# Attention and a gated feed-forward layer on one core: seven half products for half of gate and value, fixed order lists, and a residual added in DRAM

## The chip, the cores and the metric

The kernel runs on one core of a Trainium2 chip. Its time is the device time of one execution in microseconds (us). The engines are TensorE (PE, with the weight loads shown apart as PEld), VectorE (DVE), ScalarE (ACT), GpSimd (POOL) and SyncE (SP). Each runs its own instructions in program order; they wait for each other through semaphores. DMAs are issued from POOL's and SP's queues.

## The reference, cut to what matters

The first half is attention over 4 batches, 8 heads, 768 tokens and 64 numbers per head. Heads 0, 2 and 6 see all earlier tokens; the others see the first four tokens and a window of 64. The second half takes the result as `x` with 3072 rows of 512 numbers:

```
a = softmax(where(mask, q @ k.T / 8, -1e9)) @ v      # per batch and head
x = a laid out as [3072, 512]
g   = x @ w_gate                                     # [3072, 1536]
val = x @ w_val                                      # [3072, 1536]
ffn = gelu(g) * val @ w_out                          # [3072, 512]
out = x + sigmoid(x @ w_res) * ffn
```

Inputs and outputs are float32. The kernel multiplies in float16 with float32 sums.

## The kernel before

The 3072 tokens are cut into six chunks of 512 (`CHUNKS`); a chunk takes four tiles of 128 tokens, from one or two batches. Each chunk passes through the same stages. Attention writes `xtok` (its rows in float32), and transposes on TensorE give `xT`, the same in float16 with the 512 features on the partitions in four groups. `gate_value` (line 1121) works through 12 blocks `f` of 128 hidden columns. For each it makes gate and value as four matmuls of 512 tokens each into one PSUM bank; ACT then takes the gelu (line 1166) and DVE multiplies it with the value (line 1168) into `hT`. `output_fast` (line 1212) makes the product with `w_out` for pairs of token tiles. It already uses Winograd's scheme: seven products of half size in place of eight, from sums of `hT` blocks that `sums` forms on DVE (line 1187, kept in `hS` and partly over `hT`), and from sums of `w_out` blocks that `weight_sums` forms once (`wt`). Partial results are copied out of PSUM (`keep`, lines 1251 and 1252), added to (`plus`, line 1257), multiplied with the gate made from `x @ w_res` by a tanh (line 1226 and `gated`, line 1281), and added to `xtok` (line 1286). SP then stores a tile of 256 KB (line 1292). The four buffers `otile` (line 508) hold these tiles from the first keep to the end of the store. Chunk 0 does part of its work in plain form.

Attention of one chunk is interleaved with the output of the chunk before it, so TensorE alternates between stages of gate and value alone and stages of the mixed kind.

Each operation is a task of a graph (`Graph`, `schedule` at line 219) with a cost, a priority and the buffers that it needs. A list scheduler runs through modelled time, picks for each engine the ready task with the best priority for which the buffers are free, and so fixes at build time the order of each engine's queue and the place of each buffer. `HINTS` changes the priority of single tasks. Some tasks (`flex`) may go to DVE or ACT. PSUM has eight banks; `P_ps` lists for each kind of use which banks it may take. Matmuls go through a helper `mm`: lines 516 and 517 are the whole array and two halves of 64 columns.

The loads of q, k (64 KB each, transposed on the way in by DMA for some chunks) and v for all batches go through the pools `qks`, `qkt`, `va`, `vs`, `q6` in batches; `qkt` holds the transposed q and k of one batch in one buffer of which there are two.

Of the kernel before, what the change touches and what calls it, by code (L numbers as in the profile page):

```python
# [4 lines left out]
NHEAD = 8  # L5
# [38 lines left out]


HINTS = (
    "3:-58.9 11:-130.04 428:854.14 430:718.61 444:2782.08 457:-821.9 460:407.45 490:4205.68 521:1522.06 "
    "591:-818.43 610:-36.63 612:486.89 613:-2965.25 619:1544.03 621:-44.07 643:467.87 644:-881 646:4.3 656:119.6 "
    "664:25.04 673:629.62 675:-109.25 695:-2674.26 696:-1856.67 703:-881.5 706:-108.75 707:714.39 708:1939.7 "
    "711:270.02 712:497.18 716:476.22 720:652.56 738:638.32 743:520.23 744:3053.24 749:514.3 750:1799.28 "  # L50
    "751:2383.53 756:521.28 762:1469.72 764:4344.87 767:2237.74 787:-603.93 815:5053.25 817:2978.67 821:1231.87 "
    "824:1484.86 836:2402.62 837:798.1 841:706.04 848:-288.52 849:2997.07 876:2751.74 906:2555.54 913:1516.93 "
    "918:2437.99 919:1519.88 924:1537.25 931:1510.23 936:2384.32 949:2443.79 955:2089.28 967:2846.74 995:-227.38 "
    "1001:29.83 1002:3171.86 1003:3180.29 1004:1146.58 1007:2686.58 1012:1781.89 1040:-803.29 1043:1907.45 "
    "1045:1028.83 1046:667.33 1050:3229.28 1051:1536.45 1053:3573.03 1056:-1823.77 1084:4090.27 1110:2454.97 "
    "1111:2597.62 1117:2808.38 1123:2507.5 1128:2481.58 1129:2529.63 1134:2508.5 1146:2434.73 1152:2779.33 "
    "1153:3034.61 1158:3861.94 1165:2795.06 1171:3076.63 1176:2997.8 1185:5989.69 1188:2243.92 1189:2528.84 "
    "1192:2789.39 1193:2537.45 1194:3836.22 1208:3021.15 1215:6294.68 1263:3219.13 1268:5037.38 1283:4420.5 "
    "1308:4756.92 1311:3513.6 1317:3517.03 1321:3052.3 1329:5930.49 1330:3507.5 1335:3508.5 1336:3519.22 "
    "1341:4624.14 1345:3444.6 1353:3516.64 1354:3538.83 1357:2761.66 1365:3787.63 1366:5173.04 1372:5102.72 "  # L60
    "1386:5438.32 1392:4014.31 1393:4933.66 1418:5146.68 1430:4133.91 1441:5428.8 1452:5127.54 1457:2188.42 "
    "1462:4595.33 1464:5711.23 1467:9389.54 1468:4425.54 ~1471:550.69 1476:5611.77 1499:4504.13 1513:6742.83 "
    "1516:5340.27 1522:4510.5 1523:4585.63 1526:3632.38 1534:4503.02 1539:4253.34 1550:4463.64 1565:7711.51 "
    "1570:4506.5 1571:5085.34 1580:2427.42 1594:2466.44 1610:9272.71 1625:3048.93 1627:6036.71 1629:6167.81 "
    "1631:5064.12 1644:6476.5 1662:4125.72 1671:5044.95 1672:7314.6 1676:4967.2 1683:6427.71 1692:9540.12 "
    "1711:7387.16 1757:5137.62 1784:5507.1 1797:5469.41 1803:7562.23 1817:7773.49 1818:7478.69 1823:7672.83 "
    "1834:7419.08 1836:10250.4 1849:7490.55 "
)

# [31 lines left out]
class Buf:  # L101
    __slots__ = ("pool", "kind", "slot", "left", "users", "war", "free_at")

    def __init__(self, pool, kind=None):
        self.pool, self.kind = pool, kind
        self.slot = None
        self.left = 0
        self.users = []
        self.war = []
        self.free_at = 0.0  # L110


class Pool:
# [14 lines left out]

    def take(self, buf, t):
        best = min(x for x in self.free if x[0] <= t)  # L130
        self.free.remove(best)
        buf.slot = best[1]
        buf.war = list(self.last[best[1]])
        self.held.setdefault(buf.kind, []).append(None)
# [9 lines left out]
class Psum:  # L144
# [23 lines left out]

    def take(self, buf, t):
        sp = self.spots(buf.kind, t)[0]  # L170
        buf.slot = sp
        for b in sp:
            self.free[b] = 1e18
        buf.war = [u for b in sp for u in self.last[b]]
        self.held[buf.kind].append(None)
# [15 lines left out]
VS_DMA = 0  # L191
LAT = {"pe": 0.20, "act": 0.10, "dve": 0.08, "pool": 0.12, "sp": 0.1}


class Graph:
# [22 lines left out]

    def schedule(self):
# [21 lines left out]
        running = []  # L241
        while left:
# [3 lines left out]
            for e in ENGS:  # L246
# [3 lines left out]
                for t in cand[e]:  # L250
# [6 lines left out]
                    key = (int(away), p_, t.seq)  # L257
                    if t.ready > now or (best is not None and key >= bkey):
                        continue
                    if t.alts and any(max(free[f], now) + t.alts[f][0] + BIAS[f] < now + t.alts[e][0] + BIAS[e] - 1e-6  # L260
                                      for f in t.alts if f != e):
                        continue
                    need = {}
                    ok = True
                    for b in t.bufs:
                        if b.slot is None:
                            if not b.pool.can(b.kind, now):
                                ok = False
                                break
# [15 lines left out]
                progressed = True  # L285
                if t.name == "g0" and warming:
# [114 lines left out]
    def emit(self):  # L401
# [31 lines left out]
        with nc.Block() as blk:  # L433
# [18 lines left out]
            def _(e):  # L452
                run("sp", e)
                for t in finals:
                    e.wait_ge(t.sem, 16)
# [6 lines left out]
def c_act(n):  # L462
    return 0.19 + n * 0.000834


def c_dve(n, rate=1.0, psum=True):
    return (0.125 if psum else 0.065) + n * 0.00104 / rate
# [6 lines left out]
def build_kernel(nc, q, k, v, w_gate, w_val, w_out, w_res, out):  # L474
# [11 lines left out]
    scratch = sb("scratch", [128, 1], FP16)  # L486
    blank = sb("blank", [128, 128], FP16)
# [4 lines left out]
    P_vs = Pool(many("vs", 2, [128, NT - 1, NHEAD, DHEAD + 1], FP16))  # L492
    P_vk = Pool(many("vk", 2, [128, 8, DHEAD + 1], FP16))
    P_qkt = Pool(many("qkt", 2, [128, 2, NPAIR, SEQ], FP16))
# [9 lines left out]
    P_hs = Pool(many("hS", 1, [128, 3, NF // 2, 2, 128], FP16))  # L504
    wt = sb("wt", [128, 4, NF // 2, 256], FP16)
    P_ga = Pool(many("gact", 4, [128, 512], FP16))
    P_sr = Pool(many("srs", 3, [128, 512], FP32))
# [5 lines left out]
    def mm(e, o, lhsT, rhs, **k):  # L513
# [8 lines left out]
        "gv": (4, one(6, 7, 5, 4, 3, 2)), "gv0": (4, one(6, 7, 5, 4)), "gvh": (4, one(7, 6, 4, 5)), "out": (2, one(6, 7)), "fin": (4, one(6, 7, 1, 0)), "warm": (1, one(7, 5)),  # L522
# [55 lines left out]

    wtok = {}

    def load_weights():
# [6 lines left out]
        for j in range(4):  # L588
# [3 lines left out]
            wtok["o", j].late = 2.2  # L592
        for nm in "gv":
            for j in range(3):
                wtok[nm, j].late = 2.2 if j else 2.0
# [8 lines left out]
    def batch(b):  # L604
        if b not in batches:
            B_ = B()
            B_.v, B_.vs, B_.vk, B_.qkt = Buf(P_v), Buf(P_vs), Buf(P_vk), Buf(P_qkt)
# [4 lines left out]
        return batches[b]  # L612

    def values(b, a, z, base, each, on_engines=False):

        BB = batch(b)
        for i in range(a, z):
            BB.vtok[i] = dma("pool", base, 0.9, (lambda i=i: lambda: at(BB.v)[:, i, :, 0:DHEAD])(),
                             v[b, :, i * 128:(i + 1) * 128, :].rearrange("h p d -> p h d"), bufs=[BB.v])
            BB.vtok[i].late = 1.6 if base < 50 else 6.0  # L620
        if a == 0:
# [9 lines left out]
            for t in BB.vktok:  # L631
                t.slack = 12.0 if b else 0.0
# [5 lines left out]
        if on_engines:  # L638
            ts = []
            for lo, hi, pr in ((1, 2, -75),) + (() if VS_DMA else ((2, 4, 130),)):  # L640
                for dst, src, off in ((0, 64, 1), (64, 0, 0)):
                    def vs(on, dst=dst, src=src, off=off, lo=lo, hi=hi):
                        def fn(e):
                            o = at(BB.vs)[dst:dst + 64, lo - 1:hi - 1, :, :].rearrange("p i h d -> p (i h d)")
                            i_ = at(BB.v)[src:src + 64, lo - off:hi - off, :, :].rearrange("p i h d -> p (i h d)")
                            return e.activation(out=o, in_=i_, func=AF.Copy) if on == "act" else e.tensor_copy(out=o, in_=i_)
                        return fn
                    n_ = (hi - lo) * 520
# [9 lines left out]
        for lo in cuts:  # L658
            hi = lo + 1 if each else z
            ts = []  # L660
            for dst, src, off in ((0, 64, 1), (64, 0, 0)):
                ts.append(G.add("sp", 1.2, (lambda lo=lo, hi=hi, dst=dst, src=src, off=off: lambda e: e.dma_start(
                    at(BB.vs)[dst:dst + 64, lo - 1:hi - 1, :, :].rearrange("p i h d -> p (i h d)"),
                    at(BB.v)[src:src + 64, lo - off:hi - off, :, :].rearrange("p i h d -> p (i h d)")))(),
# [7 lines left out]
    def loads_rows(c, si, b, a, z):  # L672
# [27 lines left out]
        per = 1 if c == 0 or n == 4 else 2  # L700
        for k_ in range(0, NPAIR, per):
            ps_ = ORDER[k_:k_ + per]
            pr = 1000 * c - 492 + ps_[0] if c else 40 * k_ - 205
            for js in (((1,), (0,)) if c == 0 else ((0, 1),)):
                scr = Buf(P_ps, "scr" if c else "scr0")
                items = [(p, jj) for jj in js for p in ps_]
# [10 lines left out]
                def ev(on, p0=ps_[0], scr=scr, j0=js[0], m=len(items)):  # L717
                    def fn(e):
                        o = at(BB.qkt)[:, :, :, lo:hi].rearrange("c j (y x) w -> c x (j y) w", x=2)[:, p0 % 2]
                        m0 = j0 * 2 + p0 // 2  # L720
                        o = o[:, m0:m0 + m, :].rearrange("c m (p j) -> c m p j", j=n)
# [5 lines left out]
                           bufs=[scr, BB.qkt], name="qkE")  # L727
# [4 lines left out]
    def loads_natural(c, si, b, a, z):  # L732
# [8 lines left out]
        for i in range(a, z):  # L741
            for j, src in ((1, k), (0, q)):
# [9 lines left out]
                for d in ds:  # L752
                    d.late = 5.0
                t = G.add("sp", 1.65, (lambda sv=sv, i=i, j=j: lambda e: e.dma_start(
                    at(BB.qkt)[:, j, :, i * 128:(i + 1) * 128], sv(), transpose=True))(), ds, base, bufs=[st, BB.qkt], dma=0.85, name="dT")
# [4 lines left out]
            if i == a:  # L760
                values(b, a, z, base, False)
        t = G.add("sp", 0.8, lambda e: e.dma_start(at(BB.q6)[0:64, :, a * 128:z * 128], at(BB.qkt)[64:128, :, 1, a * 128:z * 128]),
                  loaded, base + 1, bufs=[BB.qkt, BB.q6], dma=0.4, name="q6")
        t.late = 1.0
        copies.append(t)
        for i in range(a, z):
            BB.q6tok[0, i] = BB.q6tok[1, i] = t
# [90 lines left out]
    def scores(P, tiles, banks, g, retr):  # L858
# [7 lines left out]
        for bi, (x, blocks, low) in enumerate(banks):  # L866
# [3 lines left out]
            for (b, kt, q0, nq) in blocks:  # L870
# [5 lines left out]
                if kt is None:  # L876
                    deps += [BB.ktok[p, q0]] + ([BB.ktok[p, q0 - 1]] if q0 else [])
                    parts = [(max(0, q0 * 128 - 64 + 64 * s), q0 * 128 + 64 * s, 64, o + 64 * s) for s in range(2)]
                else:
                    deps.append(BB.ktok[p, kt])  # L880
                    parts = [(kt * 128, q0 * 128, nq * 128, o)]
                for i in range(nq):
                    P.where[x, kt, b, q0 + i] = w_ + i * 128
                for (k0, qq, w, oo) in parts:
                    mms.append((lanes[lane], len(mms), BB, half, k0, qq, w, oo, low))
# [5 lines left out]
        def sc(e):  # L891
            side = lambda BB, low, j: at(BB.q6)[:, j, :] if low else at(BB.qkt)[:, j, p, :]
            return [e.matmul(at(scr)[:, oo:oo + w], lhsT=side(BB, low, 1)[half, k0:k0 + 128],  # L893
                             rhs=side(BB, low, 0)[half, qq:qq + w], start=True, stop=True)
                    for (_, _, BB, half, k0, qq, w, oo, low) in mms]
# [549 lines left out]
```

The softmax here doesn't subtract the row's maximum and nothing guards it: scores larger than these inputs give would overflow.

## Time and profile before

| what | value |
| --- | --- |
| median of three runs | 265.6 us (265.23, 265.60, 265.98) |
| span of the profiled execution | 263.7 us; the page gives no other time for it, so the median of the runs lies 1.9 us above its span |
| TensorE busy | 257.7 us (98%), 3226 instructions |
| VectorE busy | 181.6 us (69%), 378 instructions |
| ScalarE busy | 147.2 us (56%), 237 instructions |
| GpSimd busy | 89.3 us (34%), 127 instructions |
| first and last gate matmul stages begin at | 19.72 us (chunk 0), 224.85 us (chunk 5) |
| stages of gate and value of chunks 1 to 5 begin at | 63.7, 105.2, 143.9, 184.3, 224.9 us |
| DMA moved | 29.22 MB |

An engine's share of the span is an average; the table of 40 slices in the profile tells where in time it lies. A row of a group gives busy time and mean of one instruction, then the idle time of the engine just before it and what ended most of it. A line of the time view gives start, duration, engine, line, operation, output and inputs. A row of a tile or of a line of code adds the time from issue of a DMA to its landing.

### The profile page before, as it was taken

To read this page: it belongs to the slowest core of one execution; us is meant where nothing else is said; L and a number is where in the kernel's file an instruction comes from. 1 tells how busy PE (TensorE), PEld (TensorE's weight loads), DVE (VectorE), ACT (ScalarE), POOL (GpSimd) and SP (SyncE) were. 2 spreads that over 40 slices of the span, in tenths; PEclk is the share of its full clock that TensorE was granted. 3 is DMA by queue.
4 is the path that set the end of the run, shared out by engine and by line. 5 is a ranking of instruction groups with operands and counts; after the bars stand their busy time and mean duration, and the time that the engine had idled before them with its cause. 6 is when DMAs were issued, how large, how long until landed. Compare 5 with 4: busy or idle time off the path is not lost.

```text
span 263.7 us, 7495 instructions
## 1 busy us (share of the span) xinstructions
PE 257.7 (98%) x3226; PEld 164.0 (62%) x3226; DVE 181.6 (69%) x378; ACT 147.2 (56%) x237; POOL 89.3 (34%) x127
## 2 busy tenths in 40 slices
PE   7999999999999999999999999999999999999993
PEld 6777655468444668544567444589655588655692
DVE  2698437798447888557898366888557689837655
ACT  2785467974244987423787242967243888233430
POOL 8999979506109973975000000000000000000003
PEclk9999999999999999999999999999999999999999
DMA  6999999999999999999996110004200004200003
GB/s 83 174 204 206 188 175 231 175 153 204 134 200 148 165 137 177 171 179 176 174 156 150 42 40 0 2 26 101 82 2 0 2 2 122 82 2 0 2 35 127
DMA packets 96513, 29.22 MB, mean 111 GB/s; under 512 B 84449, under 2 KB 93025, under 8 KB 96481
## 3 DMA queue, kind: packets, MB, share of 16 engines
q0 software_dynamic: 70320, 14.69, 67.5%
q1 hardware_dynamic: 26160, 14.07, 28.0%
q8 instruction: 25, 0.41, 0.7%
q14 instruction: 8, 0.06, 0.1%
HBM read 29.36 MB, written 6.29 MB: 135 GB/s over the span
## 4 chain that ended last, share of the span: by engine, by line
PE 95%; DMA 2%; DVE 1%; issue 0%; POOLq 0%
PE ps L516 50%; PE ps L517 32%; PE ps L893 5%; PE ps L1333 2%; PE ps L1017 2%; PE ps L709 2%; DMA qks<-in_q_dram 2%; PE ps L1106 2%; PE ps L984 1%; DVE otile L1281 1%; DVE otile L1286 1%; DVE otile L1257 0%; POOLq L1427 0%
## 5 line engine op out<-in xcount | busy, mean ns | idle before, releaser
L1166 ACT ACTIVATE gact<-ps 128x512 f16<-128x512 f32 x68 | 40.2, 597 | 73.5 <-PE ps L516 43.7
L1168 DVE SCALAR_TENSOR_TENSOR hT<-gact,ps 128x512 f16<-128x512 f16 x68 | 46.1, 686 | 48.0 <-PE ps L516 23.1
L516 PE MATMUL ps<-xT,wg 128*128 128x512 f16 (+1 forms) x208 | 50.0, 363 | 0.0
L516 PE MATMUL ps<-xT,wv 128*128 128x512 f16 (+1 forms) x202 | 49.0, 362 | 0.0
L1286 POOL TENSOR_TENSOR otile<-otile,xtok 128x256 f32<-128x256 f32 x3 | 2.4, 801 | 136.2 <-DVE otile L1281 136.2
L577 POOL DMA_DIRECT2D qks<-in_k_dram x36 | 28.0, 810 | 17.3 <-DMA qkt<-qks 13.9
L516 PEld LDWEIGHTS ps<-xT,wg 128*128 128x128 f16 x208 | 20.1, 98 | 20.0 <-DVE otile L1257 0.3
L516 PEld LDWEIGHTS ps<-xT,wv 128*128 128x128 f16 x202 | 19.4, 98 | 20.0 <-DVE hT L1168 0.5
L577 POOL DMA_DIRECT2D qks<-in_q_dram x36 | 28.4, 828 | 2.2 <-issue 1.4
L517 PE MATMUL ps<-xT,wv 128*64 128x512 f16 x204 | 28.3, 380 | 0.0
L577 POOL DMA_DIRECT2D va<-in_v_dram x24 | 21.3, 920 | 15.1 <-PE ps L516 15.1
L517 PE MATMUL ps<-xT,wg 128*64 128x512 f16 x192 | 26.3, 379 | 0.0
L909 ACT ACTIVATE ea<-ps 128x1024 f16<-128x1024 f32 (+2 forms) x24 | 21.1, 915 | 1.7 <-PE ps L893 1.6
L1257 DVE TENSOR_TENSOR otile<-otile,ps 128x256 f32<-128x256 f32 x33 | 13.6, 417 | 7.1 <-PE ps L517 4.7
L1226 ACT ACTIVATE srs<-ps 128x512 f32<-128x512 f32 x22 | 13.1, 595 | 9.1 <-PE ps L517 6.7
L517 PEld LDWEIGHTS ps<-xT,wv 128*64 128x64 f16 x204 | 11.5, 110 | 9.8 <-DVE hT L1168 0.3
L1084 DVE TENSOR_TENSOR xtok<-ps,rcp 128x512 f32<-128x512 f32 (+1 forms) x28 | 16.8, 606 | 0.2
L517 PEld LDWEIGHTS ps<-xT,wg 128*64 128x64 f16 x192 | 11.1, 110 | 9.0
L893 PE MATMUL ps<-qkt 64*128 64x64 f16 (+4 forms) x391 | 16.4, 213 | 0.0
L893 PEld LDWEIGHTS ps<-qkt 64*128 64x128 f16 x391 | 9.8, 94 | 8.0 <-issue 4.2
L516 PE MATMUL ps<-wo,hT 128*128 128x256 f16 (+1 forms) x84 | 14.4, 304 | 0.0
L1286 DVE TENSOR_TENSOR otile<-otile,xtok 128x512 f32<-128x512 f32 (+1 forms) x21 | 14.3, 691 | 0.2
(109 smaller groups left out, 437.4 us busy)
## 6 DMA issues: line engine op xcount, KB each, us to landing
out_dram<-otile SPq DMA_DIRECT2D x22, 256.0 KB, 2.4
va<-in_v_dram POOLq DMA_DIRECT2D x24, 128.0 KB, 17.6
qks<-in_k_dram POOLq DMA_DIRECT2D x32, 64.0 KB, 12.6
qks<-in_q_dram POOLq DMA_DIRECT2D x32, 64.0 KB, 13.0
wg<-in_moe_w_gate_dram POOLq DMA_DIRECT2D x3, 512.0 KB, 10.2
wv<-in_moe_w_val_dram POOLq DMA_DIRECT2D x3, 512.0 KB, 12.1
wo<-in_moe_w_out_dram POOLq DMA_DIRECT2D x4, 384.0 KB, 22.8
vs<-va SPq DMA_DIRECT2D x4, 260.0 KB, 7.9
```

The lines of the kernel that those rows point to most:

```text
L516: return e.matmul(o, lhsT=lhsT, rhs=rhs, **k)
L517: return [e.matmul(o[h:h + 64], lhsT=lhsT[:, h:h + 64], rhs=rhs, **k) for h in (0, 64)][-1]
L577: return G.add(eng, issue, lambda e: e.dma_start(out_ap(), in_ap), deps, prio, bufs=bufs, dma=cost, name=name, grp=grp)
L709: return [e.transpose(out=at16(scr)[64 * x:64 * x + 64, (m * n + i) * 128:(m * n + i + 1) * 128], in_=piece(jj, h, i), identity=ident[:, : ...
L893: return [e.matmul(at(scr)[:, oo:oo + w], lhsT=side(BB, low, 1)[half, k0:k0 + 128], rhs=side(BB, low, 0)[half, qq:qq + w], start=True, sto ...
L909: return e.activation(out=o, in_=i_, func=AF.Exp, scale=SM_SCALE)
L1084: t2 = G.add("dve", c_dve(2 * n * 64), lambda e: e.tensor_tensor(out=xview(), in0=avv(0, DHEAD), in1=scale(), op=ALU.mult), [t1] + xdeps, ...
L1166: ta = G.add("act", c_act(512), (lambda gb=gb, ga=ga: lambda e: e.activation(out=at(ga)[:, :], in_=at(gb)[:, :], func=AF.Gelu))(), [tg], p ...
L1168: th = G.add("dve", c_dve(512), (lambda vb=vb, ga=ga, f=f: lambda e: e.scalar_tensor_tensor(out=hv(f), in0=at(ga)[:, :], scalar=0.5, in1=a ...
L1226: tas.append(G.add("act", c_act(512), (lambda rb=rb, sr=sr: lambda e: e.activation(out=at(sr)[:, :], in_=at(rb)[:, :], func=AF.Tanh, scale ...
L1257: return G.add("dve", c_dve(256), lambda e: e.tensor_tensor(out=dst(), in0=dst(), in1=at(D)[:, 0:256], op=ALU.add), [t, k], pr, bufs=[D, o ...
L1286: fn = (lambda ot=ot, lt=lt, w=w: lambda e: e.tensor_tensor(out=at(ot)[:, w], in0=at(ot)[:, w], in1=at(xbuf)[:, lt, w], op=ALU.add))()
```

## The change

The scheme of seven half products that `output_fast` uses for `w_out` is also used for half of gate and value in chunks 1 to 5. Blocks 6 to 11 form pairs (6,9), (7,10), (8,11), for gate and for value: six products per chunk. The left side is `xT` cut into two halves of 256 tokens and two halves of 256 features, the right side a pair of weight blocks. In place of 16 matmuls of 256 tokens (8 of 512) a pair takes 14 matmuls of 256 tokens. The partial results lie in a "lane", two neighbouring PSUM banks; there are three lanes. A product is a chain of groups of matmuls (`t15`, `t6`, `t7`, `t23`, `t4`), two copies (`seed` in PSUM, `hold` to an `otile` buffer) that may go to DVE or ACT, and two additions on DVE (`merge`). Gelu and product then read both halves. Four sums of `xT` per chunk (`xS`) and eight sums of weights, once (`gv_sums`), are made on DVE.

Further parts:

- `PLAN` holds an explicit order of the tasks for each of the five engines and a place for each buffer; the scheduler follows it and no longer uses `HINTS`. Costs in the model (`c_act`, `c_dve`) have other numbers.
- In chunks 1 to 4 (`ACCUM`) `x` is stored by SP (`store_x`, 1 MB per chunk in one DMA), and the gated tiles are added to it in DRAM by accumulating DMAs on POOL's queue. The 16 DVE adds and 16 SP stores of these chunks go. Chunk 5 adds on the chip as before, and chunk 0 too.
- `qkt` becomes `kT` per batch and `qT` per chunk; a copy `q6` on SP becomes two. `vs` no longer holds head 0. `wt` has three slabs in place of four, `srs` two buffers in place of three. `hS` is split in two. Warm-up matmuls on a zero tile at the start are 256 wide in place of 128.
- In the built program TensorE loses 240 matmuls of 512 columns and gains 420 of 256. DVE instructions go from 378 to 452, ACT from 225 to 281, POOL from 123 to 141, SP from 80 to 73.

The core of the diff:

```diff
+NP = 3
+FA, FB = NF - 2 * NP, NF - NP
+LANES = 3
-HINTS = ( ... )
+PLAN = ( ... )
+ACCUM = range(1, 5)
...
+        lists = [[int(x) for x in line.split()] for line in "".join(PLAN).split("/")] if PLAN else []
+        queue = {e: [self.tasks[x] for x in xs] for e, xs in zip(ENGS, lists)}
...
+                b.fixed = x if x >= 0 else None
...
+                offers = cand[e]
+                if queue:
+                    offers = [t for t in queue[e][heads[e]:heads[e] + 1] if t in offers] + [t for t in offers if t.name == "warm"][:1]
...
-    P_qkt = Pool(many("qkt", 2, [128, 2, NPAIR, SEQ], FP16))
+    P_kt = Pool(many("kT", 2, [128, NPAIR, SEQ], FP16))
+    P_qt = Pool(many("qT", 2, [128, NPAIR, 512], FP16))
...
+        "lane": (LANES, [(4, 5), (2, 3), (0, 1)]),
...
+    def fast(c, xtbuf, xttoks, h, toks, hv, lanes_):
...
+        s1 = add(lambda: S(0), lambda: A(1, 0), lambda: A(1, 1), ALU.add, xd, [xs, xtbuf])
+        s2 = add(lambda: S(1), lambda: S(0), lambda: A(0, 0), ALU.subtract, [s1] + xd, [xs, xtbuf])
+        s3 = add(lambda: xs3[:, :, :], lambda: A(0, 0), lambda: A(1, 0), ALU.subtract, xd + xs3_last, [xtbuf])
+        s4 = add(lambda: S(2), lambda: A(0, 1), lambda: S(1), ALU.subtract, [s2] + xd, [xs, xtbuf])
...
+            lane = lanes_[q % LANES]
+            ps, free = lane
+            es = Buf(P_ot)
...
+                    mm(e, at(ps)[:, D], lhsT=right[r](k), rhs=left[l](k), start=first and k == 0, stop=(k == 1), skip_group_check=True)
+                    for l, r, D, first in parts for k in range(2)], need + deps, p_, bufs=[ps, xtbuf, xs] + list(extra), name=name)
...
+            t15 = product([("A11", "B11", AL, True), ("S1", "T1", AR, False)], list(free))
+            seed = copy((lambda ps=ps: at(ps)[:, BL]), (lambda ps=ps: at(ps)[:, AL]), [t15], [ps], "seed")
+            hold = copy((lambda es=es: at(es)[:, 0:256]), (lambda ps=ps: at(ps)[:, AR]), [seed], [ps, es], "hold")
+            t6 = product([("S2", "T2", BL, False)], [seed])
+            m1 = merge(AR, [t6, hold])
+            t7 = product([("S3", "T3", BL, False)], [m1])
+            t23 = product([("A12", "B21", AL, False), ("S4", "B22", AR, False)], [m1])
+            m2 = merge(BR, [t7])
+            t4 = product([("A22", "T4", BL, False)], [m2])
...
+    def store_x(c, xbuf, xtoks):
+        n = 2 if c == len(CHUNKS) - 1 else 4
+        r0 = c * 512
+        stored[c] = G.add("sp", 0.65, lambda e: e.dma_start(
+            out[r0:r0 + n * 128, :].rearrange("(i p) d -> p i d", p=128), at(xbuf)[:, 0:n, :]),
...
+            if c in ACCUM and not end:
+                t = G.add("pool", 1.0, (lambda ot=ot, r0=r0: lambda e: e.dma_start(out[r0:r0 + 128, :], at(ot)[:, :], accum_op=ALU.add))(),
+                          ends + [stored[c]], pr - 3000, bufs=[ot], dma=1.0, name="out")
+                continue
```

## The prediction

> **What bounds the kernel now.** I read the page first (shares, slices, chain), then the busy time of each engine stage by stage, then the order of TensorE's work in time, then how long DMAs take from issue to landing.
>
> ```profile
> span 263.7 us, 7495 instructions
> PE 257.7 (98%) x3226; PEld 164.0 (62%) x3226; DVE 181.6 (69%) x378; ACT 147.2 (56%) x237; POOL 89.3 (34%) x127
> PE   7999999999999999999999999999999999999993
> PEclk9999999999999999999999999999999999999999
> DMA  6999999999999999999996110004200004200003
> ...
> PE 95%; DMA 2%; DVE 1%; issue 0%; POOLq 0%
> ...
> L1257 DVE TENSOR_TENSOR otile<-otile,ps 128x256 f32<-128x256 f32 x33 | 13.6, 417 | 7.1 <-PE ps L517 4.7
> ...
> out_dram<-otile SPq DMA_DIRECT2D x22, 256.0 KB, 2.4
> ```
>
> TensorE is busy in every slice but the first and last, at the full granted clock, and the chain that ends last is 95% TensorE. The DMA engines are full for the first 21 of 40 slices (to about 138 us) and nearly idle afterwards: DMAs added early meet a full queue, those added late do not.
>
> Busy time by stage: columns are window, length, then PE, PEld, DVE, ACT, POOL with counts, clock, DMA share, GB/s. The first is attention of chunk 2 with output of chunk 1, the second gate and value of chunk 5.
>
> ```profile
> 84.80:105.20 20.40, 20.37 (x300) 14.21 (x300) 17.17 (x40) 17.35 (x25) 14.72 (x21) 1.00 2.05 155
> 224.90:246.70 21.80, 21.80 (x216) 12.12 (x214) 13.71 (x23) 7.14 (x13) 0.00 (x0) 1.00 0.07 26
> ```
>
> In the gate/value stage TensorE has no gap and VectorE 8.1 us to spare. The time view (start, duration) gives the price of a matmul:
>
> ```profile
> 225.99 1.03 PE L517 MATMUL ps<-xT,wg 128*64 128x512 f16 x8
> 226.86 0.60 PE L517 MATMUL ps<-xT,wv 128*64 128x512 f16 x4
> ...
> 246.71 1.89 PE L517 MATMUL ps<-wr,xT 128*64 128x512 f16 x16
> 248.44 0.82 PE L517 MATMUL ps<-wo,hT 128*64 128x256 f16 x12
> 249.09 0.82 PE L517 MATMUL ps<-wt,hS 128*64 128x256 f16 x12
> 249.75 0.60 PE L517 MATMUL ps<-wr,xT 128*64 128x512 f16 x4
> ```
>
> From 225.99 to 246.71 lie the 96 matmuls (each two half-width instructions) of 12 blocks: 20.72/96 = 0.2158 us per 512-wide matmul. Six 256-wide ones take 249.75 − 249.09 = 0.66, or 0.109 us each. Halving the width halves the time, so half products cost no extra by themselves.
>
> **The change part by part.**
>
> *Half products.* In chunks 1 to 5 gate and value of blocks 6–11 form six products per chunk; each replaces 16 half-width-equivalent pieces (8 matmuls of 512) by 14 of 256. The built order agrees: 240 matmuls of 512 go, 420 of 256 come. 240 × 0.2158 = 51.8; 420 × 0.1092 = 45.9. On the path: **−5.9 us**, 1.18 per chunk. [...] But the matmuls start at a constant pitch proportional to their width, with nothing waited for between them; weight loads lie beside them. So I take −5.9, not 0.
>
> *What the products ask of the other engines.* Each product (a "lane" of two PSUM banks) is now a chain: t15, seed copy, t6, merge, t7, merge, t4, and only then gelu or h. With TensorE-to-ACT/DVE hand-off 0.21 us (last matmul of wr issued, to tanh at 247.78), 0.06 back, ACT 256-wide 0.38, a merge 0.42 (the row of L1257, the same form with output in an otile): 0.44+0.21+0.38+0.06+0.22+0.21+0.42+0.06+0.22+0.21+0.42+0.06+0.22+0.21 = 3.3 us to the end of t4, about 4.5 with two gelus (0.60 each, starting 0.49 apart), 4.7 with two h. Three lanes do two rounds each: 9.2 us. TensorE has 6 × 1.53 = 9.2 us in the products and 5.2 us in blocks 3–5 to interleave. In the built order between g6's t15 and t6 stand g4, g4, v6, g7: 1.74 us against 0.65 needed. The tightest place is v8 before t23: 0.655 of cover against 0.69. Walking chunk 5 by hand gives some 0.2 us of stalls. But it assumes VectorE free at each hand-off. It gets per chunk 12 merges (at 0.34–0.42: 4.1–5.0), 4 xS sums of 512 f16 (0.34–0.42: 1.4–1.7), and about two seed/hold copies (0.8): 6.3–7.5 on top of 13.71 = 20.0–21.2, in a stage that should be 21.8 − 1.2 = 20.6. The cover is thus nearly gone; a merge that queues behind an h (0.69) is late by up to 0.69, and next late is t7 or t4 on TensorE, which has no other order to take. Ends: 0 (hand walk) and 1.25 per chunk (DVE's overshoot at 97% fill, 21.9 − 20.6), 6 in all. I take 0.3 per chunk, **+1.5**, near the hand walk since it uses measured rows. ACT gets 28 seeds and 21 holds over five chunks, some 3.7 us per chunk, on 7.14 of 21.8: covered. The eight weight sums of DVE (at most 0.95 each, the time of a wt sum of twice the elements) fall into chunk 0 and 1's stages, where DVE has 8 us free (13.06 of 21.10).
>
> *Addition in DRAM.* For chunks 1–4, 16 adds of DVE (0.69 each, 2.7 us per chunk) go; they lie beside TensorE in the attention/output stages (DVE 17.17 of 20.40), so 0 on the path, unless they were what held a wait there. Instead SP issues four 1 MB stores of x, and POOL 16 accumulating stores of 256 KB, each about 1 us of POOL's queue. Queued behind them on POOL are the 64 KB loads of q and k of batches 2 and 3; behind the x store on SP are row transposes of chunk 2 and copies of q6. Their own slack is 1–3 us or more. The otile buffer (4 of them, now also used by the products' holds) comes free only when the accumulation has landed, where before it waited for an SP store.
>
> The trace has no accumulating DMA. The place that decides is the first tile of chunk 1, stored during attention of chunk 2: a keep of ACT takes that buffer 6.55 us after issue, and TensorE needs that keep about 1.3 us later. Landing times in that stage:
>
> ```profile
> L1292 SPq DMA_DIRECT2D out_dram<-otile x2: 347/468/588, 96.2 to 99.2; - x2
> DMA to landing us min/median/max: 6.1/6.5/6.9
> ...
> L577 POOL DMA_DIRECT2D qks<-in_k_dram x5: 790/827/858, 83.3 to 89.2; - x5
> DMA to landing us min/median/max: 7.0/7.8/9.1
> ```
>
> [...] The rows of the loaded stage show 6.1 to 9.1, and the rows win. On them: 6.5 gives no stall, 7.8 none (the 1.3 us absorb it), 9.1 gives 1.3, and 12.6 (the page's median of all k loads, early ones among them) 4.7. A second marginal place is a store of chunk 1 queued behind loads on POOL, taken by a hold of chunk 2 (about 112 to 120 us). Stores of chunks 3 and 4 meet an idle DMA (2.4 us). Ends 0 and 5; I take **+1.0**, nearest to the POOL row. A gain below nothing is excluded: no buffer comes free sooner than by a plain store.
>
> *Order lists, fixed places, split qkT.* The floor of a chunk by matmul pitch is 20.8 (gate, value) + 3.5 (wr) + 9.2 (w_out) + 5.4 (attention) = 38.9; the stages stand 38.7 to 41.5 apart, so up to 1.6 us per chunk are short waits within attention, which another order can save or double. Ends −2 and +2; taken at 0.
>
> *Start.* A few transposes of chunk 1 come before the first gate matmul (+0.57), warm-up matmuls on the blank tile between the first transposes and that point become 49 at 0.109 in place of 83 at 0.06 (+0.3), and row transposes taken four pairs at once return 0.4. A 256 KB load and one v load move ahead of the weights, about 2.2 us of POOL's queue; wg landed at 16.9 for a use at 19.72, so 19.1 for 20.3; later slabs keep 1.4 us or more. **+0.5**; ends 0 and +1.5 (first slab late).
>
> *Tail.* Chunk 5 still adds on the chip and stores by SP; from the last matmul to the end 4.2 us remain. 0.
>
> Sum: −5.9 + 1.5 + 1.0 + 0 + 0.5 + 0 = −2.9. The profiled span 263.7 becomes 260.8; the median of the runs, 265.6, lies 1.9 above the span (what lies around it), so **262.7**.
>
> **Rivals.**
>
> *Clean saving* (0.20). Lanes and buffers never wait: −5.9 + 0.5 − 0.7 for better filled attention = −6.1, 259.5. For it: the hand walk. Against: DVE's sum at the brim.
>
> *VectorE sets the pace of the gate/value stage* (0.15). Middle overshoot 0.9 per chunk, 4.4 in all: −5.9 + 4.4 + 1.0 + 0.5 = 0, 265.6, no change. For it: 20.0–21.2 of 20.6. Against: xS sums can run ahead of the stage.
>
> *Accumulating stores land late* (0.20), the slower side. [...] It decides from about 7.9 us of landing at the first place. At 12.6, 4.7 us there; the second and third place have some us more slack and lose 1 each: −5.9 + 1.5 + 0.5 + 4.7 + 2 = +2.8, 268.4. For it: full DMA until 138 us; against: TensorE's wait so far for plain stores is small.
>
> *The change does not do what it says*: excluded by the counts of the built order.
>
> **How the numbers follow.** The likeliest case (0.45) lies at 262.7, its own range 260.5 to 264.5. With the clean case below and DVE's case above, and the late-store case's lower part, 8 in 10 lie in 258.8 to 267.2. A difference of 0.3% is 0.8 us, about what measurement tells from no change: faster is under 264.8, slower above 266.4. Faster 0.42 + 0.20 + 0.04 = 0.66; same 0.03 + 0.07 + 0.01 = 0.11; slower 0.04 + 0.19 = 0.23.
>
> **What would show it.** In the profile after: PE's busy time down by about 5.9; gate/value stages of chunks 1–5 at about 20.6 where now 21.8 (20.9 would be the lane waits), with DVE above 19 of it; idle time before PE's product lines released by DVE merges under 2 us in all. Accumulating stores of chunk 1 landing in 7–9 us and those of chunks 3–4 in 2–3.5; idle of ACT before keep or hold ended by a DMA near 95–100 us would be the late-store case. If PE's pitch for 256-wide products exceeds 0.12 us, or DVE's merges exceed 0.5 us, the sum is wrong.

## Result and the profile after

The change makes no difference that the runs can tell: 266.29 us median (264.71 to 269.30, 20 runs) against 265.78 (265.23 to 266.78, 20 runs), ratio 1.002 with the interval 0.9998 to 1.0042. The forecast was 262.7. The spread is a result of its own: 4.6 us where the kernel before has 1.6. The profiled execution was one of the longer ones (267.75 us, span 265.8), 2.1 us above the profiled span before. The page after, with the lines that answer to those of before:

```profile
span 265.8 us, 8070 instructions
PE 255.9 (96%) x3425; PEld 184.4 (69%) x3425; DVE 204.2 (77%) x452; ACT 165.0 (62%) x293; POOL 106.6 (40%) x145
PE   8999999999999999999999999999999996999991
PEclk9999999999999999999999999999999997999997
DMA  6999999999998979999999999209700265150003
...
PE 92%; DVE 3%; ACT 2%; issue 1%
...
L1523 POOL DMA_DIRECT2D out_dram<-otile x16 | 14.6, 988 | 85.9 <-DVE otile L1519 83.2
L1366 DVE TENSOR_TENSOR ps<-ps,otile 128x256 f32<-128x256 f32 x60 | 24.7, 429 | 9.8 <-PE ps L616 4.2
...
out_dram<-xtok SPq DMA_DIRECT2D x4, 1024.0 KB, 6.5
out_dram<-otile POOLq DMA_DIRECT2D x16, 256.0 KB, 5.3
```

TensorE's row, solid before, has a 6 in the 34th of 40 slices, and the granted clock a 7 under it; the DMA row, nearly empty in the last third before, has bursts there. The waits of TensorE (total, times, longest) name the hole, and the time view shows it in the last attention stage:

```profile
PE ps L617 <- issue: 2.3, 1, 2.3
PE ps L1578 <- DVE blank L650: 1.1, 1, 1.1
PE ps L616 <- DVE wS L1414: 0.2, 1, 0.2
PE ps L1226 <- DVE x L1202: 0.2, 1, 0.2
```

```profile
219.87 0.26 PE L617 MATMUL ps<-vk,ek 128*64 128x65 f16 x5
222.45 0.32 PE L617 MATMUL ps<-vk,ek 128*64 128x65 f16 x3 [2.32 <-issue]
...
223.38 1.52 PE L617 MATMUL ps<-wo,hT 128*64 128x256 f16 x12
```

No wait on a lane, on a merge or on an otile buffer is in the list: what the prediction feared most does not show. Instead TensorE stands 2.3 us for "issue", that is, for nothing that the profile shows, in the middle of eight like matmuls. Then twelve half-width `w_out` matmuls take 1.52 us where twelve took 0.82 before. The columns below are window, length, busy times of PE, PEld, DVE, ACT and POOL with counts, then the granted clock, DMA share and GB/s. A packet counts whole in the window where it starts, so the share can exceed 1. Hardly an engine works in the hole, the DMAs do, and after it the clock is halved.

```profile
220.10:222.40 2.30, 0.03 (x2) 0.00 (x0) 0.33 (x1) 0.00 (x0) 0.00 (x0) 0.95 1.23 130
222.40:225.60 3.20, 3.15 (x39) 3.16 (x41) 1.32 (x3) 0.90 (x2) 0.00 (x0) 0.50 0.02 5
```

Where the 2.1 us come from. I added up TensorE's time, from the start of each record to the next, by what the matmuls multiply. Gate and value fall from 125.1 to 119.5, **−5.6**. Attention goes from 42.9 to 45.8, **+2.9**: the hole is 2.3 of it. The `w_out` products go from 58.1 to 60.9, **+2.8**, with 1.4 from the halved clock (75 instructions took 2.90 us there and 1.51 in a run without a hole). Warm-up +0.7, `w_res` −0.5. Together TensorE ends 0.4 later, at 259.9 where it was 259.5. The rest of the span, from there to the end, grows from 4.2 to 5.9: **+1.7**.

### The profile page after: what moved, and what is told of

It reads as the page before. It is cut to its first block, busy times and chain, and to the rows that moved or that the text cites. A ratio compares the mean times of both kernels' runs of the same rounds, so it can differ in the third digit from the quotient of the medians.

```text
span 265.8 us, 8070 instructions
## 1 busy us (share of the span) xinstructions
PE 255.9 (96%) x3425; PEld 184.4 (69%) x3425; DVE 204.2 (77%) x452; ACT 165.0 (62%) x293; POOL 106.6 (40%) x145
## 4 chain that ended last, share of the span: by engine, by line
PE 92%; DVE 3%; ACT 2%; issue 1%
PE ps L616 45%; PE ps L617 31%; PE ps L1013 5%; PE ps L1578 4%; PE ps L1137 2%; PE ps L824 2%; PE ps L1226 2%; ACT gact L1384 1%; DVE hS L1414 1%; ACT srs L1463 1%; PE ps L1104 1%; DVE otile L1519 1%; DVE hT L1391 0%; ACT L1111 0%; DVE wS L1414 0%
## 5 line engine op out<-in xcount | busy, mean ns | idle before, releaser
L1523 POOL DMA_DIRECT2D out_dram<-otile x16 | 14.6, 988 | 85.9 <-DVE otile L1519 83.2
L678 POOL DMA_DIRECT2D qks<-in_q_dram x36 | 33.2, 991 | 15.6 <-DMA qT<-qks 14.8
L616 PE MATMUL ps<-xT,wg 128*128 128x512 f16 (+1 forms) x172 | 38.0, 337 | 0.0
L616 PE MATMUL ps<-xT,wv 128*128 128x512 f16 (+1 forms) x168 | 37.8, 336 | 0.0
L1366 DVE TENSOR_TENSOR ps<-ps,otile 128x256 f32<-128x256 f32 x60 | 24.7, 429 | 9.8 <-PE ps L616 4.2
L616 PE MATMUL ps<-wo,hT 128*128 128x256 f16 (+1 forms) x114 | 19.5, 296 | 0.2 <-DVE wS L1414 0.2
L617 PE MATMUL ps<-xT,wv 128*64 128x512 f16 (+1 forms) x152 | 19.6, 346 | 0.0
L617 PE MATMUL ps<-xT,wg 128*64 128x512 f16 (+1 forms) x144 | 18.0, 344 | 0.0
L1013 PE MATMUL ps<-qT,kT 64*128 64x64 f16 (+4 forms) x391 | 16.6, 213 | 0.1
L1362 ACT ACTIVATE ps<-ps 128x256 f32<-128x256 f32 x28 | 10.3, 371 | 9.8 <-PE ps L616 7.1
```

Of the source, the lines that this page charges most:

```text
L616: return e.matmul(o, lhsT=lhsT, rhs=rhs, **k)
L617: return [e.matmul(o[h:h + 64], lhsT=lhsT[:, h:h + 64], rhs=rhs, **k) for h in (0, 64)][-1]
L678: return G.add(eng, issue, lambda e: e.dma_start(out_ap(), in_ap), deps, prio, bufs=bufs, dma=cost, name=name, grp=grp)
L1013: return [e.matmul(at(scr)[:, oo:oo + w], lhsT=side(BB, qb, low, 1)[half, k0:k0 + 128], rhs=side(BB, qb, low, 0)[half, qq:qq + w], start=T ...
L1366: return G.add("dve", c_dve(256), lambda e: e.tensor_tensor(out=at(ps)[:, o], in0=at(ps)[:, BL], in1=at(es)[:, 0:256], op=ALU.add), deps, ...
```

## The experiments

Two things had to be explained: the hole with its spread, and the tail. The first theory came from the trace's DMA records. On a queue q8, "instruction", the page has blocks of 16 KB (27 after, 25 before), which I read as TensorE's instructions. In the profile before, 122 to 379 of them, matmuls and weight loads together, lie between two fetches, 252 on average (251 after), so a block holds about 250; the expectation of the shifted program takes 256. Ahead of the hole, 479 passed, and the block then arrived at 221.1 us. By the pace of the other blocks it was due near 217 us, and from 215.1 to 221.0 the records are full of packets of three accumulating stores of chunks 3 and 4. So: **the accumulating stores fill the DMA engines, the fetch waits, and TensorE runs out of instructions.** The rivals: DMA transposes of `xT` hold the fetch; the place in the program waits for something unseen; the price lies in the landing of the stores.

**The changed kernel again (again).** No edit.

> The changed kernel once more, unedited. Its profiled span of 265.8 us held one gap of 2.3 us on TensorE (220.1 to 222.4, released by nothing but issue) followed by a halved granted clock until 225.6. Theory A (the gap is a late fetch of TensorE's instructions that comes and goes): times between 264.7 and 269.3 again, median near 266.3; if this profile has no gap its span is 261.5 to 263, if it has one 265 to 266. Theory B (the gap belongs to the order of the program, every time the same): the gap is in this profile too, at the same place and of the same length within 0.3 us, and the times lie within 1 us.

265.22 us (264.33 to 267.28), ratio to before 0.9977 (0.9961 to 0.9992). The profile has a hole at the same instruction, the 5825th of TensorE's stream, but 1.9 us long in place of 2.5 (from start to start), and no halved clock after it; the fetch began at 218.4, not at 220.2. That is neither of the theories as written: the place is fixed and the length comes and goes. The granted clock of the single runs agrees: in the 20 runs of the result six had 0.989 to 0.991, all of them at 267.75 us or more, and of these 22 none was under 0.993.

**Plain stores (plain16).** All 16 stores of chunks 1 to 4 without the addition; `x` is missing in those rows.

```diff
-e.dma_start(out[r0:r0 + 128, :], at(ot)[:, :], accum_op=ALU.add))(),
+e.dma_start(out[r0:r0 + 128, :], at(ot)[:, :]))(),
```

> The 16 accumulating stores of chunks 1 to 4 become plain stores (accum_op left out), so x is not added for those rows; all else is as in the changed kernel. Theory A1 (TensorE's instruction fetch is held up behind the packets of the accumulating stores): no gap over 1 us on TensorE, median 264.5 to 265.0, spread of the times under 1.5 us as for the kernel before. Theory A2 (the fetch is held up by the DMA transposes of xT, or by the plain amount of instructions): gap and spread stay, median 266 to 266.5. Rival on the landing (the prediction's late stores): the landing of these stores falls from 5.3 us (median) to 2.5 to 4 and idle of ACT or DVE before keep and hold falls with it by over 1 us; I expect under 0.3 us of that.

263.28 us (263.14 to 263.45, 4 runs), ratio 0.9898 (0.9881 to 0.9914): 1.9 us under the changed kernel measured beside it, with a spread of 0.3 us in its four runs. The hole at the 5825th instruction is gone. The groups of DMA records in one stretch show why; first the changed kernel, then this one:

```profile
DMA packets 426, 0.74 MB, mean 106 GB/s; under 512 B 66, under 2 KB 66, under 8 KB 426
...
q0 software_dynamic: 397, 0.74, 75.7%
q1 hardware_dynamic: 29, 0.01, 0.5%
```

```profile
q0 software_dynamic: 240, 0.79, 30.1%
q1 hardware_dynamic: 532, 0.14, 9.7%
q8 instruction: 1, 0.02, 1.0%
```

Both are 213 to 220 us; columns are packets, MB and the share of 16 engines' time. About the same 0.75 MB from POOL's queue take 76% of the engines' time as accumulating packets of 2 KB and 30% as plain ones of 4 KB. The plain run has an instruction block in that stretch (it began at 216.9, after 269 instructions); the changed kernel has none. The transposes of `xT`, one of the rivals, go through SP's queue q1: the plain run moves 532 of its packets in this stretch and still has no hole. The landing fell from 5.3 to 2.8 us, but ACT and DVE had no DMA wait before keep or hold to lose: the landing was not the price.

**Chunk 4 on the chip (chip4).** DVE adds `x` in chunk 4 (the new tasks stand behind the last gated in DVE's list), plain stores there.

```diff
+                if c in CHIP:      # CHIP = (4,)
+                    onchip.append((t, ends, ot, xbuf, lt, xtoks[lt], pr))
...
+        a = G.add("dve", c_dve(512), ... out=at(ot)[:, :], in0=at(ot)[:, :], in1=at(xbuf)[:, lt, :], op=ALU.add) ...)
+        t.deps = t.deps + [a]
```

> Only chunk 4, whose accumulating stores lie at the gap: x is added by DVE on the chip (four adds of 128x512 right behind the last gated of each tile) and the store is plain; the 1 MB store of x of chunk 4 shrinks to one row, which is overwritten. Theory A1: the gap near 220 us is gone, median 264.5 to 265.3 (four adds of 0.69 us on DVE beside TensorE), though gaps at chunks 2 to 4 can remain. Theory A2: gap and median (266 to 266.5) as in the changed kernel.

266.78 us, ratio 1.0028 (1.0016 to 1.0040). The hole was 1.0 us, not gone: one accumulating store of chunk 3 stands among those of chunk 4 in POOL's list, its packets filled 217.4 to 219.5, and the fetch began at 219.4. And the adds are not free: TensorE's waits now name DVE.

```profile
PE ps L620 <- issue: 0.8, 1, 0.8
PE ps L1140 <- issue: 0.6, 1, 0.6
PE ps L1140 <- DVE eb L1068: 0.5, 1, 0.5
PE ps L620 <- DVE hT L1297: 0.5, 1, 0.5
PE ps L620 <- DVE otile L1523: 0.4, 1, 0.4
```

**Shorter warm-up (warm).** The first 24 warm-up matmuls 176 wide.

```diff
-e.matmul(at(warm)[:, 0:256], lhsT=blank[:, 0:128], rhs=blank[:, :], ...)
+e.matmul(at(warm)[:, 0:w_], lhsT=blank[:, 0:128], rhs=blank[:, 0:w_], ...)   # w_ = 176 if i_ < 24 else 256
```

> The first 24 warm-up matmuls are 176 columns wide in place of 256. In the changed kernel they keep TensorE until 6.37 us, where the first transposes of q began at 5.68 before. Theory S (the in-order warm-up delays the start): the first transposes begin at 5.6 to 5.8, the first gate matmul at 20.4 to 20.7 in place of 21.18, time 0.5 to 0.7 us under that of the unedited kernel of this call. Theory W (the first gate matmul waits for weights or for the later attention chain only): the first transposes come earlier but the first gate matmul stays at 21.0 to 21.3, and the time does not change by over 0.3 us.

A miss on both. The transposes began at 5.77 as theory S has it, but the full clock was granted only at 10.1 us (4.3 to 7.1 in the profiles of the change and its variants with the warm-up as made, 4.2 before), the first gate matmul came at 22.17, and the time was 267.04. In this profile the shorter warm-up loses in the clock what it saves in the queue; whether it does so in every run, one profile cannot tell. The median has another part: nine of the 22 runs have a granted clock of 0.989 to 0.991, as the two profiles with a halved clock behind the hole, and take 267.25 us or more. Why they are more here than in the unedited kernel stays open.

**The same program, shifted by 122 instructions (shift).** This is the sharpest test: behind the warm-up no DMA, no operand and no width changes, only the position of the block boundaries.

```diff
+e.matmul(at(warm)[:, o_:o_ + 256 // n_], lhsT=blank[:, 0:128], rhs=blank[:, 0:256 // n_], ...)
+            for o_ in range(0, 256, 256 // n_)      # n_ = 2 from the 13th warm-up on
```

> The warm-up matmuls from the 13th on are issued as two of 128 columns in place of one of 256: the same columns, but some 122 more TensorE instructions (matmul and weight load) before the first gate matmul. Everything after is the same program. In the changed kernel the gap began in three profiles at the 5825th TensorE instruction, inside the small matmuls of the last attention stage, and the instruction fetch of 16 KB before it began late. Theory A (instructions come in blocks of 256 and the gap stands where a block ends while the fetch of the next is held up): the gap leaves its matmul and stands some 122 instructions earlier in the program, near 218 to 219 us, again close to the 5825th instruction of the stream, 1 to 4 us long. Theory D (the gap belongs to that place of the program, a wait that the trace doesn't show): the gap stays before the same vk,ek matmuls (now near the 5947th instruction).

The hole moved. It stands again at the 5825th instruction of the stream, but inside `va,ea` matmuls, 122 instructions earlier in the program; the fetch before it began at 220.0, after 490 instructions. The last three columns are operands, tile and count:

```profile
219.05 0.77 PE L617 MATMUL ps<-va,ea 128*64 128x65 f16 x38
222.25 0.73 PE L617 MATMUL ps<-va,ea 128*64 128x65 f16 x34 [2.43 <-issue]
```

A wait that belonged to the program would have stayed before the `vk,ek` matmuls. 267.30 us, ratio 1.0042 (1.0021 to 1.0062): it is no cure. In the changed kernel 252 instructions of TensorE take 2.9 to 5.3 us in this stretch (211 to 220 us), and the packets of the accumulating stores fill more than that (216.0 to 223.3 us here). The hole of 2.6 us, like that of 2.5, was followed by 3.41 us at half clock; those of 1.0 to 1.9 us were not.

**Late stores (late, late_b).** Three stores of chunk 4 wait for the first gate matmul of chunk 5, where 252 instructions last 7.8 to 10.7 us in the changed kernel (226 to 247 us); the one of chunk 3 goes ahead of them.

```diff
+    for t in held[1:]:                       # three stores of chunk 4
+        t.deps = t.deps + [ph(5, "gv")[0][1]]
-1376 1580 1583 1373 1612 1609
+1376 1373 1580 1583 1612 1609
```

> The accumulating stores stay, but three of the four of chunk 4 wait for the first gate matmul of chunk 5 (about 225 us), where TensorE uses 256 instructions in some 10 us and not in 4, and one of chunk 3 that stood among them on POOL goes ahead of them. Theory A1 (accumulating packets hold up the fetch): no gap at the 5825th instruction, the fetch near 217 us starts at once; time 1.5 to 2.5 us below the changed kernel, 263.0 to 264.0, as with plain stores (263.3). If the price of the accumulating stores is in something else (their landing, POOL's queue), the time stays at 265 to 266. Risk: a hold of chunk 5 waits for these stores, up to 1 us.

264.19 us (263.44 to 266.23), ratio **0.9933** (0.9912 to 0.9955). No hole; the fetch began at 217.9 after 269 instructions. In TensorE's waits nothing is longer than the start:

```profile
PE ps L1581 <- DVE blank L650: 1.1, 1, 1.1
PE ps L616 <- DMA xT<-x: 0.2, 1, 0.2
PE ps L616 <- DVE wS L1414: 0.2, 1, 0.2
PE ps L1226 <- DVE x L1202: 0.2, 1, 0.2
```

The stores still accumulate, DVE still has no adds; only their time was moved. Run again:

> The late stores of chunk 4 once more, on the same chip as the combined kernel, so that the two are compared under one roof: 264.0 to 264.4, no gap at the 5825th instruction in this profile either. If the absence of the gap was luck of one profile, a gap of 1 to 2.5 us is back and the time is 265 or more.

263.48 us (263.23 to 263.77, 4 runs), ratio 0.9907 (0.9882 to 0.9931), no hole at the 5825th instruction. Another hole, of 0.8 to 1.2 us at 58 us in chunk 0's stage, is in this and most other profiles of the new program. In the shifted program it stayed at its matmul, so it does not go with the count of instructions; its cause was not tried.

**The third part undone (chip16).** All 16 adds on DVE, plain stores from POOL.

```diff
-CHIP = (4,)
+CHIP = (1, 2, 3, 4)
```

> All 16 tiles of chunks 1 to 4 are added on the chip by DVE (16 adds of 128x512 behind the last gated of their tile), stored plainly from POOL's queue, and the 1 MB stores of x shrink to a row each: the third part of the change undone, with lanes and order lists kept. Theory A1 alone: as plain16, 263.3 plus nothing. Theory V (DVE is full in the attention stages as well, where these adds stand; chip4 with four of them gave 266.8 in spite of a gap of only 1.0 us): 0.7 to 2 us per chunk, 266 to 270.

267.35 us, ratio 1.0052 (1.0035 to 1.0069). There is no hole at that place, and yet it is the slowest median of all: the list of TensorE's waits has 2.6 us for DVE, where the changed kernel has 0.4 behind the start. So theory V holds in its lower half. The accumulating stores earn their place by keeping 16 adds off DVE; they were only issued where they did harm. This holds for these lists: the adds were put into an order made without them, and an order made for them was not tried.

**The tail (tail, tail2).** First SP's order of the last stores, then also the place of one add (from POOL's list to DVE's, behind task 1816).

```diff
-1822 1851 1858 /
+1851 1858 1822 /
```

> At the end SP's last three stores are reordered: the two halves that GpSimd adds finish (ready at 261.7) go ahead of the one that waits for DVE's last add (262.2), where the changed kernel issued them behind it, at 262.6 and 263.1. Theory T (the two stores queued behind are part of the longer tail, 6.0 us after the last matmul against 4.4 before): the end comes 0.5 to 0.9 us earlier, at the same chip as the changed kernel 0.4 to 0.9 us under it in the floor of its times. Theory U (the landing of the last DVE-added store sets the end): no change.

265.28 us. The median does not tell it from the unedited kernel (ratio to before 0.9971 against 0.9977), since the hole is still there (1.7 us in this profile). What shows the edit is the span after the last matmul, 5.3 us where it was 5.9: the two stores queued behind were worth 0.6.

```diff
-1609 1850 1855 1856 1817 1849 /
+1609 1850 1855 1856 1849 /
-1816 1819
+1816 1817 1819
```

> On top of the reordered last stores, the 512-wide add of the tail goes from GpSimd to DVE, into the 0.47 us in which DVE waits for the last tanh. In the changed kernel the gated product beside that GpSimd add took 1.15 us where the same form takes 0.42. Theory P (the two engines hinder each other there): the gated product is back at 0.42 us, the tail after the last matmul is 4.6 to 5.0 us (6.0 in the changed kernel, 5.4 with the stores reordered alone), floor of the times 0.3 to 0.5 us under that of the stores alone (263.92). Theory Q (the product was long for another reason): it stays above 1 us and DVE, with 0.69 us more to do, ends later.

264.61 us (from 263.20), tail 4.8. DVE's time view at the end, the changed kernel first:

```profile
259.94 1.15 DVE L1519 SCALAR_TENSOR_TENSOR otile<-srs,otile 128x256 f32<-128x256 f32 x1 [0.47 <-ACT srs L1463]
261.02 0.41 DVE L1519 SCALAR_TENSOR_TENSOR otile<-srs,ps 128x256 f32<-128x256 f32 x1
```

```profile
257.93 0.69 DVE L1529 TENSOR_TENSOR otile<-otile,xtok 128x512 f32<-128x512 f32 x1
258.54 0.42 DVE L1519 SCALAR_TENSOR_TENSOR otile<-srs,otile 128x256 f32<-128x256 f32 x1
```

The gated product of 256 columns with both inputs in SBUF is back from 1.15 to 0.42 us once no add of GpSimd runs beside it (259.55 to 260.81 in the changed kernel). A part of it only moved: the 512-wide gated before it took 1.26 beside another GpSimd add.

**Both (best).** Late stores and both edits of the tail.

> The late stores of chunk 4 together with the two edits of the tail. If the two parts are independent: 264.2 (late alone) less 1.0 to 1.3 (6.0 us of tail to 4.7) gives 262.9 to 263.2, 1.0 to 1.2% under the kernel before; no gap at the 5825th instruction. If the tail is bound by something else, 263.6 or more.

262.75 us (262.25 to 263.65, 5 runs) against 265.98, ratio **0.9882** (0.9857 to 0.9907). Measured beside it, the late stores alone gave 263.48 and the edits of the tail alone 264.61. Its longest run, 263.65, is shorter than the shortest of either kernel (264.33 of the changed one, 265.16 of the one before). It is the change as made, with three entries of its lists moved and one wait added.

```profile
span 260.9 us, 8069 instructions
...
PE   8999999999999999999999999999999999999992
PEclk9999999999999999999999999999999999999999
```

## Why the prediction was wrong, step by step

The step that failed is the price of the accumulating stores: it was looked for in buffers, and it lay in TensorE's instruction fetch. Two terms put at 0, the tail and the order lists, cost 2.9 us more. With the terms as measured the sum is −5.6 + 0 + 1.9 + 1.7 + 1.2 + 0.5 = −0.3 us, and the two medians of the changed kernel lie at +0.5 and −0.8. That 266.29 lies within the wide range given, 258.8 to 267.2, is luck: no rival named this cause.

- **Half products, −5.9: right.** The trace has −5.6 for gate and value, chunk 0 included. (The stage of 21.8 us in the prediction began with `w_out` matmuls; the gate and value matmuls of a chunk alone go from 20.7 to 20.9 us to 19.6 to 19.8.) The pitch of 256-wide products stays at 0.109 us, while weight loads are busy for 69% of the span where it was 62%; the 0 that the prediction weighed against −5.9 did not occur.
- **Lanes, +1.5: too much.** TensorE never waited for a seed, hold or merge by more than 0.2 us. A merge took 0.429 us as assumed, but DVE had more room in the gate/value stage than the sum gave it: 14.1 of 19.8 us from 227.6 to 247.4, where 20.0 to 21.2 was forecast. Work that I had left in the stage is no longer there: the sums of `hT` (2.8 us), which now follow it, two adds of chunk 4 (1.3), which the change itself took away, and the last `xtok` and `xT` copies (1.1). The rival in which VectorE sets the pace there did not occur. Where DVE has no room for more is the attention stage, as chip16 shows (2.6 us of TensorE's waits are for DVE).
- **Accumulating stores, +1.0: the price was put in the wrong place.** I asked when they land and which buffer waits. They landed in 5.3 us (3.8 to 8.2; those of chunks 3 and 4 in 3.8 to 7.2, where 2 to 3.5 was forecast), no wait for a buffer is in the list, and the rival of late stores, as I had written it, did not occur. What they cost is the DMA engines' time: 1.9 us by plain16. I had costed the stores of chunks 3 and 4 at nothing because the DMA was "nearly idle" there. It is idle of data, but one small transfer in it is on the path: TensorE's instructions, which the page lists as q8 with 0.7%. In the profile before, the list of TensorE's waits has 1.1 us for the start, 0.7 us for a load of q and nothing for "issue", so its 25 fetches cost nothing that shows. In seven profiles of the new program and its variants a late fetch cost 1.0 to 2.6 us.
- **Tail, 0: wrong, +1.7.** I took the same form for the same cost. Two stores behind a later one are 0.6 of it, a GpSimd add beside a gated product 0.4. The other 0.7 stays in the tail of the last version; 12 matmul instructions follow the last `w_res` product where 24 did, 0.66 us less beside the tanh that waits for it, but that was not tried.
- **Order lists, 0: +1.2 or so.** With late stores, attention, `w_out` and `w_res` together take 1.2 us more of TensorE than before (123.9 against 122.7). Four waits, at the same four matmuls in all twelve profiles of the new program and its variants, come to about that much. The list of waits gives them 0.2 us or nothing, but from start to start they lose 0.43 (for DVE's `x`), 0.38 (for its `wS`), 0.27 (for ACT's `srs`) and 0.26 (for DVE's `hT`) against the plain pitch of the matmul before. Two of them, in the last version:

```profile
131.25 0.38 PE L616 MATMUL ps<-wt,wS 128*128 128x256 f16 x2
131.85 0.38 PE L616 MATMUL ps<-wo,hT 128*128 128x256 f16 x2 [0.21 <-DVE wS L1414]
...
181.06 0.49 PE L617 MATMUL ps<-wt,hT 128*64 128x256 f16 x6
181.77 0.44 PE L1226 MATMUL ps<-ident,x 128*64 128x128 f16 x9 [0.21 <-DVE x L1202]
```

  Whether the order, the fixed places or DVE's fuller queue makes them was not tried. The prediction's "up to 1.6 us per chunk" did not follow from its figures either: 38.7 to 41.5 against a floor of 38.9 is −0.2 to 2.6.
- **Start, +0.5:** 0.4 to 1.5 in the profiles with the warm-up as made (first gate matmul at 20.1 to 21.2 us), of which 0.2 to 0.8 are left when chunk 1's gate stage is under way. Right in size.

With the hole and part of the tail mended the kernel gives 262.75, which is what the sum said; but errors of opposite sign (lanes and stores against order lists and rest of the tail) help it there, so this is in part luck and no proof of the sum.

## What to carry to other kernels

An idle DMA is not a free DMA: here TensorE's own instructions came over it (q8, 0.7% of its time), and a burst of accumulating stores in a stretch of many small matmuls (76% of the engines' time from 213 to 220 us) starved it for 1.0 to 2.6 us. When a trace has idle time on "issue" at a fixed count of instructions, compare the times of the instruction queue's packets; then move the burst to where instructions last longer, which was worth about 1 us here (264.19 against 265.22). A forecast for a tail needs the order of each queue at the end, not only the form of the work.

## What was not expected of the hardware

- After a fetch landed, TensorE went on only 1.3 to 1.6 us later (seven profiles). In the changed kernel the fetch ahead of the hole began at 220.2 us, some 3 us late, took 0.97 us, and TensorE went on at 222.4.
- Accumulating stores into DRAM go in 2 KB packets of 0.178 us, plain ones in 4 KB packets of 0.171 (medians at 213 to 220.5 us, changed kernel and plain16): half the rate, and a median landing of 5.3 against 2.8 us.
- TensorE's clock was halved for 3.41 us after holes of 2.5 and 2.6 us (from start to start; 2.3 and 2.4 us without a matmul) and not after 1.0 to 1.9.
